# Two transformer-like layers on one core: free VectorE time for waiting shift adds, and two more joined gelus

## The chip, the cores and the metric

The kernel runs on one core of a Trainium2 chip. The metric is the device time of one execution in microseconds (us), the median of several runs. The engines are named as in the profile: PE (TensorE), PEld (its weight loads), ACT (ScalarE), DVE (VectorE), POOL (GpSimd) and SP, which here only issues DMAs.

## The reference

The input x is 2048 rows of 512 in bf16. Four blocks are applied, A, B, A, B, with the same weights both times; A and the B after it are called a layer, so there are layer 0 and layer 1.

```python
x = x + A(layernorm(x), wq, wk, wv, wo)
x = x + B(layernorm(x), w1, w2, w3, w4)      # and both once more

def A(x, ...):       # 32 query heads of 16, one key head and one value head
    q = (x @ wq) in 32 heads; k = x @ wk; v = x @ wv
    p = softmax(q @ k.T / 4)
    return (p @ v, heads side by side) @ wo

def B(x, ...):
    h = gelu(layernorm(x) @ w1)
    hs = (four quarters of h, shifted by 1, -1, 2, -2 rows) @ w2
    x1 = x + hs
    return x1 + gelu(layernorm(x1) @ w3) @ w4      # w3: 512 x 1792, w4: 1792 x 512
```

The exponentials are the bulk: 2 layers x 32 heads x 2048 x 2048 of them.

## The kernel before, in words

**Tiles and chunks.** The 2048 rows are 16 tiles of 128. Queries go in chunks (`CHUNKS`): four of 4 tiles in layer 0; 4, 4, 4, 2 and 2 tiles in layer 1. A chunk is written (layer, number). The scores of one half of a block of four heads against one block of keys are a "half", 128 partitions by 1024 numbers; there are 2048 of them in all, 1024 to a layer.

**Two ways for a half.** As a *unit* (`declare_unit`): PE makes two banks of scores (L1127), ACT takes exp of them (L1170), and PE multiplies by the values (`add_pv`, L1281). As a *pair* (`declare_pair`): PE makes two banks, one after the other, and DVE turns each into the bits of an approximate exponential with a multiply and add into a 16-bit integer (L1190). The approximation is the weighted sum of three such exponentials, J, J + 43 and J + 86 in integer steps (`STEP`). The additions are *shifts* (L1227): a `tensor_scalar` on 16-bit integers in SBUF, which POOL or DVE can do. A shift usually does two rows at once, the second term of the newest pair and the third term of the one before, 2048 numbers per partition. PE then makes three value passes for a pair, where a unit has one. There are `N_J` = 5 J slots.

**Side work.** All else is side work: projections, layer norms, the mixer (W1, gelu, W2) and the MLP (W3, gelu, W4). It is declared for a whole chunk when the last half of the chunk is done (`chunk_end`) and is spread under the next chunk's halves. `PACE` sets how densely its matmuls may begin.

**The gelus.** ACT holds one set of functions at a time, so it loads a table between exp and gelu. A chunk has two gelu episodes, one after W1 (L1586) and one after W3 (`gelus`, L1681), each a load, the gelus and a load back. For a chunk in `JOINED`, `mlp` stops behind W3 and remembers itself in `self.kept`; the next chunk's `mixer_in` then runs its own gelu and the kept one in one episode, and only afterwards declares the kept chunk's W4 matmuls (`mlp_out`) and the layer norm, keys and values that they allow for layer 1 (`next_kv`). Before, three chunks of layer 1 are joined and none of layer 0.

**Layer 0 to layer 1.** Layer 1's first chunk begins on the keys it has: 7 blocks against key tiles 0 to 5, then 6 to 10 (`EARLY`), with partial sums put aside. The rest waits for the last rows of layer 0. The queries of (1,0) and (1,1) are made by `qproj`, whose copies go through SP's queue.

**The order.** Nothing is scheduled on the chip. While the kernel is built, a planner (`Plan`) plays the execution through: each operation has a duration (`dur`), a priority (lower goes first) and predecessors. Whenever an engine is free in that play, `_pick` chooses an operation that is ready, and `_place` puts it at the end of the engine's list. On the chip, each engine then runs its list in order with semaphore waits. The planner's figures (latencies `LAT`, `DRAIN`, durations, `port` for the SBUF port that DVE and POOL share) thus decide the order and nothing else. `roll` is its idea of PE's clock: it looks at activity in windows of 3.4133 us. `MOODS` are sets of rules (how eager pairs and side work are); the string `TEMPER` names one mood for each stretch of 12.5 us of the play.

**Where a shift goes.** `shift_op` decides when the shift is declared, often before it can start: if the rows that POOL has been given and that are not yet placed sum to less than `ADDS` (4, in some moods 5 or 6), POOL gets it, else DVE. A shift on DVE takes the place of its pair in `self.pairs`, on which `assign` counts unfinished pairs (`MAX_PAIRS`, 2) before it gives another half to DVE. 

Of the kernel before, what the change touches and what calls it, by code (L numbers as in the profile page):

```python
# [27 lines left out]
class Op:  # L28
    __slots__ = ("eng", "emit", "preds", "npend", "succ", "dur", "prio", "seq", "ready", "start",
                 "end", "take", "give", "dma", "out", "pos", "sem", "vc", "side", "placed", "pe", "feeds", "port", "parts", "after", "entry", "weight", "qop")  # L30


class Plan:
# [4 lines left out]

    LAT = {"PE": 0.06, "ACT": 0.045, "DVE": 0.045, "POOL": 0.1, "SP": 0.1}

    DRAIN = {"ACT": 0.15, "DVE": 0.085, "POOL": 0.0}
    SELF = 0.035
    MARGIN = 0.15
    SWITCH = 0.103
    WAVE = 0.006
    WINDOW = 3.4133
    WARM = 0.40
    STAY = 0.36
# [22 lines left out]
    LEAD = 0.4  # L71
    JOIN = 0.7
    LEFT = 1
    HORIZON = 1.0

    def __init__(self, nc, pool_banks):
# [32 lines left out]
    def op(self, eng, emit, reads=(), writes=(), dur=0.1, prio=None, take=None, give=None,  # L109
# [7 lines left out]
        o.after = after  # L117
        o.feeds = o.qop = None
        o.seq = len(self.ops)
# [75 lines left out]
    def roll(self, t):  # L195
        w = int(t / self.WINDOW)
        while self.window < w:
            ask = self.STAY if self.warm else self.WARM
            self.warm = self.activity[-1] >= ask * self.WINDOW * 2400.0
            self.window += 1  # L200
            self.activity.append(0.0)
# [7 lines left out]
    def _pick(self, eng, t, dense=False):  # L209
# [66 lines left out]
        if o.take is not None:  # L276
            got = bank
            self.pool = [x for x in self.pool if x[1] not in got]
            o.take.bank = got[0] if o.take.n == 1 else got
            for b in got:  # L280
                last = self.pool_last.get(b)
                if last is not None:
                    o.preds.add(last)
        return o

# [89 lines left out]
    def _place(self, o, t):  # L375
# [14 lines left out]
        elif o.eng == "PE":  # L390
# [11 lines left out]
            o.dur = end - t  # L402
            o.end = end + 0.17
            self.free_at["PE"] = t + 0.015 if len(o.pe) > 3 else end
# [39 lines left out]
    def run(self, pump):  # L444
        while True:
            if not self.events:
                if pump(self.now):
                    continue
                break
            t = heapq.heappop(self.events)  # L450
            while self.events and self.events[0] <= t + 1e-9:
                heapq.heappop(self.events)
            self.now = max(self.now, t)
            again = True
            while again:
                again = pump(self.now)
                for e in ENGINES:
                    if self.free_at[e] <= self.now + 1e-9:
                        o = None
                        if e == "PE" and self.now >= self.pe_end - 1e-9 and self.idle():  # L460
                            o = self._pick(e, self.now, dense=True)
                            if o is None:
                                self.filler()
                        if o is None:
                            o = self._pick(e, self.now)
                        if o is None and e == "PE" and self.now >= self.pe_end - 1e-9 and self.left \
                                and self.filler is not None:
                            heapq.heappush(self.events, self.now + 0.25)
                        if o is not None:
                            self._place(o, self.now)  # L470
                            again = True
# [107 lines left out]
class Kernel:  # L579
# [12 lines left out]
    STEP = 43  # L592
    ADDS = 4
    PARTS = (0.3203125, 0.25390625, 0.201171875)
# [3 lines left out]
    CALM_END = (2, 1)  # L598
    JOINED = ((1, 0), (1, 1), (1, 2))
    LATE_OT = 6  # L600
# [15 lines left out]
    MOODS = (  # L616
        (0.55, 3.0, 1.0, 3.0, 0.45, 0.7, 2, 4, 0.0),
        (0.53, 2.5, 0.8, 3.0, 0.45, 0.7, 2, 5, 0.0),
        (0.57, 3.5, 1.2, 3.3, 0.45, 0.7, 2, 4, 8.0),
        (0.52, 3.0, 1.5, 2.0, 0.6, 0.7, 2, 5, -6.0),  # L620
        (0.55, 2.0, 1.0, 3.0, 0.3, 1.0, 2, 4, 0.0),
        (0.55, 4.0, 0.7, 4.0, 0.45, 0.5, 2, 4, 0.0),
        (0.55, 3.0, 1.0, 3.0, 0.45, 0.7, 1, 4, 20.0),
        (0.55, 3.0, 1.5, 2.5, 0.6, 1.0, 3, 5, -15.0),
        (0.60, 3.0, 0.6, 3.0, 0.2, 0.4, 2, 4, 0.0),
        (0.50, 2.7, 1.1, 2.8, 0.5, 0.8, 2, 4, 0.0),
        (0.55, 3.0, 1.0, 3.0, 0.45, 0.7, 2, 4, 20.0),
        (0.55, 1.0, 1.0, 3.0, 0.45, 0.7, 2, 4, 0.0),
        (0.55, 3.0, 1.0, 3.0, 0.45, 0.7, 2, 5, 0.0),
        (0.55, 3.0, 1.0, 3.0, 0.45, 0.7, 2, 4, -15.0),  # L630
        (0.55, 3.0, 1.5, 3.0, 0.7, 1.2, 3, 6, 0.0),
        (0.57, 2.0, 1.0, 2.0, 0.45, 1.0, 3, 4, 0.0),
    )
    TEMPER = "2007ee7feefe3e77397e7f0ef710ef7e7137eeeef85cf427784ffe15048005003909f1eef04f7ef7e3eee8e77574e04e701e0f9515e5bef20000"

# [293 lines left out]
    def ln_in(self, la, tiles, prio=None):  # L929
# [6 lines left out]
        for part in self.portions(tiles):  # L936
            self.stats(src, part, lambda tb: ("X", tb), prio)
            self.rstd(part, prio)
            for tb in part:
                self.apply(base[0][:, tb % 4, :], src(tb), tb, [("X", tb)], [(base[1], tb % 4)],  # L940
                           0.355, prio)
            n0 = (part[0] % 4) * 128
# [212 lines left out]
    def declare_unit(self, g):  # L1155
# [8 lines left out]
        def fpe(e):  # L1164
            ins = None
            for j, h in enumerate(hs):
# [5 lines left out]
                                                       ACTF.Exp, scale=0.25),  # L1172
                         writes=[L, ("EA", ea)], dur=0.06 + 1024 / 1200, prio=0, side=False, give=L)
        o.qop = q
# [48 lines left out]
    def shift_op(self, d, f, rows):  # L1223
# [5 lines left out]
            reads=[t for r in rows for t in self.jtag(r - 1)], writes=[t for r in rows for t in self.jtag(r)],  # L1229
            dur=t_x4(1024 * n) if eng == "DVE" else 0.27 + 0.853 * n, prio=2, side=False, port=True,  # L1230
            after=0.0 if eng == "DVE" else 0.07)
        if eng == "DVE":
            self.pairs[-1] = o
        else:
            o.weight = n
            self.adds.append(o)

# [126 lines left out]
    def scale_pair(self, k, n, fin):  # L1364
# [6 lines left out]
        def fx(e):  # L1371
# [11 lines left out]
            self.RZ[:, :, b0:b0 + 2, :].rearrange("p i b z -> p (b z) i").unsqueeze(3).to_broadcast([128, 16, 2, 16])),  # L1383
           reads=[("RZ", b0), ("RZ", b0 + 1)], writes=[("RZE",)], dur=0.72, prio=fin, port=True)
        op("PE", fx, reads=[("RZE",), ("ID",)], writes=[M], pe=tiled(n), prio=fin, take=M)
# [160 lines left out]
    def mixer_in(self, la, c, tiles, tail):  # L1546
# [4 lines left out]
        for part in self.portions(tiles):  # L1551
            self.stats(lambda tb: self.X[:, tb, :], part, lambda tb: ("X", tb), None)
            self.rstd(part, None, both=True)
            for tb in part:
                self.apply(self.Y[:, tb % 6, :], self.X[:, tb, :], tb, [("X", tb)], [("Y", tb % 6)], 0.355, None)
                op("POOL", lambda e, tb=tb: e.tensor_scalar(
                    out=self.ZR[:, tb % 4, :], in0=self.Y[:, tb % 6, :], scalar1=self.SM[:, 1, tb:tb + 1],
                    scalar2=0.0, op0=ALU.mult, op1=ALU.add),
                   reads=[("Y", tb % 6), ("R2", tb)], writes=[("ZR", tb % 4)],
                   dur=0.71, prio=self.QUICK, port=True)  # L1560
            i0 = part[0] - tiles[0]
# [71 lines left out]
    def mlp(self, la, tiles, tail):  # L1633
# [12 lines left out]
        for tb in tiles:  # L1646
            op("POOL", lambda e, tb=tb: e.tensor_tensor(out=self.X[:, tb, :], in0=self.Y[:, tb % 6, :],  # L1647
                                                       in1=self.X[:, tb, :], op=ALU.add),
               reads=[("Y", tb % 6)], writes=[("X", tb)], dur=1.3, port=True)
        for f in range(14):  # L1650
# [97 lines left out]
```

## Time and profile before

| | us |
|---|---|
| median of 3 runs | 1467.19 |
| lowest and highest | 1467.02, 1468.6 |
| profiled execution, its own time | 1468.02 |
| its span from first to last instruction | 1466.2 |

| engine | busy us | share of the span |
|---|---|---|
| PE | 1436.7 | 98% |
| ACT | 1398.3 | 95% |
| DVE | 1306.2 | 89% |
| POOL | 1119.0 | 76% |

ACT runs 1401 exps, DVE 1294 halves of pairs (647 pairs) and 153 shifts, POOL 526 shifts. ACT has 26 table loads of 1.283 us each. The mean granted clock of PE is 0.994; two stretches ran at half clock.

A line of the groups gives the source line, engine, operation, what is written and read, and the count; then the time in which the group was busy, the mean length of one in ns, and the idle time just ahead of its members with what ended it. A line of the waits gives who waited, for whom, the total in us, how often, and the longest. In the windows each engine's busy time is followed by its instruction count.

### The profile page before, as it was taken

How to read it: one execution, taken by the hardware profiler on the slowest of the kernel's cores; microseconds unless marked ns; L12 is line 12 of the kernel's file. 1: busy time of each engine (PE TensorE's matmuls, PEld its weight loads, DVE VectorE, ACT ScalarE, POOL GpSimd, SP SyncE). 2: the span in 40 equal slices, each digit the busy share in tenths (PEclk: the TensorE clock that was granted, in tenths of full speed). 3: DMA queues.
4: the chain of work that ended last, by engine and by line, in shares of the span. 5: the costliest groups of instructions: out<-in, count | busy, mean ns of one | idle time of the engine just before them, and what ended most of it. 6: DMA issues, size and time to landing. Idle time of an engine off the chain costs nothing.

```text
span 1466.2 us, 64989 instructions
## 1 busy us (share of the span) xinstructions
PE 1436.7 (98%) x29592; PEld 637.1 (43%) x29592; DVE 1306.2 (89%) x2350; ACT 1398.3 (95%) x1487; POOL 1119.0 (76%) x822
## 2 busy tenths in 40 slices
PE   8999999999999999999999999999999999999999
PEld 3344334444334444434444444444444444545555
DVE  8999999999899989999987889999998998988863
ACT  7999999999899999999989999999999999999952
POOL 2878888888789879887874689878887888868741
PEclk9999999999899999999999999999999999999999
DMA  6100100001000000000000000010000000000000
GB/s 218 26 10 5 20 6 6 7 5 20 6 4 7 6 5 6 16 10 4 3 3 3 3 10 11 6 20 5 6 14 13 8 6 14 7 14 13 9 15 24
DMA packets 32660, 21.73 MB, mean 15 GB/s; under 512 B 13056, under 2 KB 31872, under 8 KB 32384
## 3 DMA queue, kind: packets, MB, share of 16 engines
q1 hardware_dynamic: 32384, 17.57, 5.2%
q8 instruction: 231, 3.78, 1.1%
q14 instruction: 45, 0.37, 0.1%
HBM read 7.90 MB, written 2.10 MB: 7 GB/s over the span
## 4 chain that ended last, share of the span: by engine, by line
ACT 62%; PE 30%; DVE 5%; POOL 2%; issue 1%; DMA 0%; POOLq 0%
ACT EA L1170 59%; PE PB L1127 9%; PE PB L720 9%; PE PB L1281 9%; DVE J L1190 2%; ACT G L1681 2%; POOL J L1227 1%; PE PB L918 1%; ACT L1170 1%; DVE ST L834 1%; PE PB L1051 1%; ACT GP L1586 1%; DVE J L1227 0%; PE PB L975 0%; DVE G L1666 0%
## 5 line engine op out<-in xcount | busy, mean ns | idle before, releaser
L1170 ACT ACTIVATE EA<-PB 128x1024 bf16<-128x1024 f32 x1401 | 1290.2, 1162 | 13.1 <-PE PB L1127 12.5
L1227 POOL TENSOR_SCALAR J<-J 128x2048 uint16<-128x2048 uint16 (+1 forms) x526 | 953.8, 1813 | 241.9 <-DVE J L1227 113.9
L1190 DVE TENSOR_SCALAR J<-PB 128x512 uint16<-128x512 f32 x1294 | 830.1, 681 | 70.1 <-PE PB L1127 65.2
L1127 PE MATMUL PB<-QT,KT 32*128 32x512 bf16 (+1 forms) x4608 | 604.8, 361 | 11.1 <-ACT EA L1170 4.1
L1281 PE MATMUL PB<-J,VD 128*32 128x256 bf16 (+1 forms) x8676 | 414.2, 265 | 7.5 <-POOL J L1227 4.1
L1281 PE MATMUL PB<-EA,VP 128*32 128x256 bf16 (+1 forms) x6324 | 355.9, 266 | 1.5 <-DVE J L1190 0.6
L1127 PEld LDWEIGHTS PB<-QT,KT 32*128 32x128 bf16 x4608 | 162.4, 91 | 384.7 <-ACT EA L1170 289.8
L1281 PEld LDWEIGHTS PB<-J,VD 128*32 128x32 bf16 x8676 | 187.6, 95 | 143.0 <-issue 94.6
L1281 PEld LDWEIGHTS PB<-EA,VP 128*32 128x32 bf16 x6324 | 145.8, 95 | 156.3 <-issue 140.4
L720 PE MATMUL PB<-ZT,W 128*32 128x512 bf16 (+2 forms) x2816 | 168.2, 342 | 0.4 <-DVE ZT L927 0.2
L1227 DVE TENSOR_SCALAR J<-J 128x2048 uint16<-128x2048 uint16 (+1 forms) x153 | 109.5, 717 | 7.1 <-POOL J L1227 6.6
L720 PE MATMUL PB<-W,G 128*32 128x512 bf16 x1624 | 104.5, 381 | 0.2 <-ACT G L1681 0.2
L1666 DVE CAST G<-PB 128x512 bf16<-128x512 f32 (+2 forms) x126 | 72.1, 579 | 11.1 <-PE PB L720 9.2
L720 PEld LDWEIGHTS PB<-ZT,W 128*32 128x32 bf16 x2816 | 63.0, 96 | 36.2 <-issue 23.5
L854 POOL TENSOR_TENSOR SM<-SM,MH 128x2 f32<-128x2 f32 (+1 forms) x69 | 50.6, 738 | 20.8 <-DVE SM L856 11.0
L1681 ACT ACTIVATE G<-G 128x1792 bf16<-128x1792 bf16 x29 | 47.0, 1684 | 19.6 <-DVE G L1666 19.6
L720 PEld LDWEIGHTS PB<-W,G 128*32 128x32 bf16 x1624 | 37.2, 96 | 39.4 <-issue 13.2
L1647 POOL TENSOR_TENSOR X<-Y,X 128x512 bf16<-128x512 bf16 x32 | 39.0, 1227 | 8.3 <-DVE Y L1629 5.8
L834 DVE BATCH_NORM_STATS2 ST<-X 128x6 f32<-128x512 bf16 x64 | 42.8, 677 | 1.6 <-DMA X<-in_A_x_dram 1.2
L1321 DVE CAST ACCF<-PB 128x512 bf16<-128x512 f32 (+1 forms) x65 | 40.0, 615 | 2.5 <-PE PB L1281 2.4
L720 PE MATMUL PB<-WO,OT 128*32 128x512 bf16 x512 | 37.8, 381 | 0.9 <-issue 0.9
L1707 DVE TENSOR_TENSOR OUTB<-PB,X 128x512 bf16<-128x512 f32 x16 | 11.0, 688 | 27.7 <-PE PB L720 27.7
(106 smaller groups left out, 745.2 us busy)
## 6 DMA issues: line engine op xcount, KB each, us to landing
OT<-ACCF SPq DMA_DIRECT2D x432, 8.0 KB, 1.8
W<-in_B_w_dram SPq DMA_DIRECT2D x2, 1792.0 KB, 15.0
X<-in_A_x_dram SPq DMA_DIRECT2D x8, 256.0 KB, 5.4
QT<-QS SPq DMA_DIRECT2D x32, 64.0 KB, 2.5
out_dram<-OUTB SPq DMA_DIRECT2D x16, 128.0 KB, 1.7
OT<-ACCF SPq DMA_DIRECT2D x112, 4.0 KB, 2.2
W<-in_B_w_dram SPq DMA_DIRECT2D x2, 512.0 KB, 9.6
WQ<-in_A_wq_dram SPq DMA_DIRECT2D x1, 512.0 KB, 4.9
```

Of the source, the lines that this page charges most:

```text
L720: ins = e.matmul(self.PB[32 * g:32 * g + 32, bank, 0:n], lhsT=lhsT[:, 32 * g:32 * g + 32], rhs=rhs, start=start, stop=stop, tile_position= ...
L834: op("DVE", lambda e, tb=tb: e.bn_stats(self.ST6[:, tb, :], src(tb)), reads=[tagf(tb)], writes=[("ST", tb)], dur=0.606, prio=prio)
L854: op("POOL", lambda e: e.tensor_tensor(out=out, in0=src, in1=self.MH[:, 0, a:b], op=ALU.pow), reads=tags + [("MH",)], writes=tg(r), dur=0. ...
L1127: ins = e.matmul(self.PB[:, bank, j * n:(j + 1) * n], lhsT=self.KT[32 * h:32 * h + 32, la, (kb + j) * 128:(kb + j + 1) * 128], rhs=self.QT ...
L1170: o = q.feeds = op("ACT", lambda e: e.activation(self.EA[:, ea, :, :], self.PB[:, L.bank[0]:L.bank[0] + 2, :], ACTF.Exp, scale=0.25), writ ...
L1190: o = op("DVE", lambda e, i=i, L=L: e.tensor_scalar(out=self.J[:, 3 * s, i * 512:(i + 1) * 512], in0=self.PB[:, L.bank, :], scalar1=128 * ...
L1227: o = self.pl.op(eng, lambda e: e.tensor_scalar(out=self.J[:, d, :], in0=self.J[:, f, :], scalar1=float(self.STEP), scalar2=1.0, op0=ALU.a ...
L1281: ins = e.matmul(self.PB[32 * x:32 * x + 32, A.bank, p * hw:p * hw + hw], lhsT=v[:, la, kb + j, :], rhs=ap[:, i, j * w + u * hw:j * w + u ...
L1321: self.last_copy = op("DVE", lambda e: e.tensor_copy(acc, self.PB[:, A.bank, 0:n]), writes=[ac] + am, dur=t_ps(n), prio=0, side=False, give=A)
L1647: op("POOL", lambda e, tb=tb: e.tensor_tensor(out=self.X[:, tb, :], in0=self.Y[:, tb % 6, :], in1=self.X[:, tb, :], op=ALU.add), reads=[(" ...
L1666: op("DVE", lambda e, f=f, L=L: e.tensor_copy(self.G2[:, f, 0:n], self.PB[:, L.bank, 0:n]), writes=[L] + [(x, f, i) for x in ("G2", "GE") ...
L1681: self.pl.op("ACT", lambda e, i=i: e.activation(self.G2[:, :, i * 128:(i + 1) * 128], self.G2[:, :, i * 128:(i + 1) * 128], ACTF.Gelu_appr ...
```

## The change

1. A new `borrow`: when DVE has nothing else to do in the planner's play, POOL is busy and the shared port comes free within `LULL` = 0.45 us, DVE takes the oldest ready shift out of POOL's queue.
2. `ADDS` goes up by 2 in every mood: POOL may be given up to 6 (or 7, 8) unplaced rows before a shift is bound to DVE.
3. `JOINED` takes in (0,0) and (0,1).
4. Planner figures: some durations, `LAT` of DVE, `DRAIN` of ACT, the end of a single bank of scores, `JOIN` from 0.7 to 1.3 (the priority at which a unit's scores that aren't urgent join others), and `roll` now moves in quarters of a window (`BINS`).
5. Another `TEMPER`; the two strings agree in 22 of 116 places.

```diff
-    LAT = {"PE": 0.06, "ACT": 0.045, "DVE": 0.045, "POOL": 0.1, "SP": 0.1}
+    LAT = {"PE": 0.06, "ACT": 0.045, "DVE": 0.05, "POOL": 0.1, "SP": 0.1}
-    DRAIN = {"ACT": 0.15, "DVE": 0.085, "POOL": 0.0}
+    DRAIN = {"ACT": 0.11, "DVE": 0.085, "POOL": 0.0}
+    BINS = 4
-    JOIN = 0.7
+    JOIN = 1.3
+    LULL = 0.45
...
     def roll(self, t):
-        w = int(t / self.WINDOW)
+        w = int(t * self.BINS / self.WINDOW)
         while self.window < w:
             ask = self.STAY if self.warm else self.WARM
-            self.warm = self.activity[-1] >= ask * self.WINDOW * 2400.0
+            self.warm = sum(self.activity[-self.BINS:]) >= ask * self.WINDOW * 2400.0
...
+    def borrow(self, t):
+        if self.free_at["POOL"] <= t + 1e-9 or self.port - t > self.LULL:
+            return None
+        h = [o for o in self.heap["POOL"] if o.flex and o.ready <= t + 1e-9]
+        if not h:
+            return None
+        o = min(h, key=lambda o: o.seq)
+        self.heap["POOL"].remove(o)
+        o.eng, o.dur, o.after = "DVE", o.flex, 0.0
+        return o
...
-            o.end = end + 0.17
+            o.end = end + (0.195 if kind == "Q" and act < 200 else 0.17)
...
                         if o is None:
                             o = self._pick(e, self.now)
+                        if o is None and e == "DVE":
+                            o = self.borrow(self.now)
...
-    ADDS = 4
+    ADDS = 6
-    JOINED = ((1, 0), (1, 1), (1, 2))
+    JOINED = ((0, 0), (0, 1), (1, 0), (1, 1), (1, 2))
...
     MOODS = (
-        (0.55, 3.0, 1.0, 3.0, 0.45, 0.7, 2, 4, 0.0),
+        (0.55, 3.0, 1.0, 3.0, 0.45, 0.7, 2, 6, 0.0),
...
-    TEMPER = "2007ee7feefe3e77397e7f0ef710ef7e7137eeeef85cf427784ffe15048005003909f1eef04f7ef7e3eee8e77574e04e701e0f9515e5bef20000"
+    TEMPER = "0184777f99f477e52777e374efe430779ef2771778570177e0083e2004000314093e49710fef799feef443873f1e0ee11705c154031407220200"
...
-            dur=t_x4(1024 * n) if eng == "DVE" else 0.27 + 0.853 * n, prio=2, side=False, port=True,
+            dur=t_x4(1024 * n) if eng == "DVE" else 0.264 + 0.859 * n, prio=2, side=False, port=True,
...
         else:
             o.weight = n
+            o.flex = t_x4(1024 * n)
             self.adds.append(o)
```

The other durations change a little: an exp from 0.06 to 0.0632 plus its 1024 / 1200, a layer norm's application from 0.355 to 0.33, and on POOL the spread of the reciprocals from 0.72 to 0.69, the second norm's scaling from 0.71 to 0.68 and the X add from 1.3 to 1.24.

## The prediction

> **What bounds the kernel now.** The order of reading was: busy shares on the page, then the windows of the span, then the waits, then the chain and the timeline at the one place where ScalarE stands still.
>
> ```profile
> PE 1436.7 (98%) x29592; PEld 637.1 (43%) x29592; DVE 1306.2 (89%) x2350; ACT 1398.3 (95%) x1487; POOL 1119.0 (76%) x822
> ...
> L1170 ACT ACTIVATE EA<-PB 128x1024 bf16<-128x1024 f32 x1401 | 1290.2, 1162 | 13.1 <-PE PB L1127 12.5
> L1227 POOL TENSOR_SCALAR J<-J 128x2048 uint16<-128x2048 uint16 (+1 forms) x526 | 953.8, 1813 | 241.9 <-DVE J L1227 113.9
> L1190 DVE TENSOR_SCALAR J<-PB 128x512 uint16<-128x512 f32 x1294 | 830.1, 681 | 70.1 <-PE PB L1127 65.2
> ...
> L1227 DVE TENSOR_SCALAR J<-J 128x2048 uint16<-128x2048 uint16 (+1 forms) x153 | 109.5, 717 | 7.1 <-POOL J L1227 6.6
> ```
>
> All four compute engines look full, so the shares decide nothing. The windows do:
>
> ```profile
> 36.00:1400.00 1364.00, 1342.22 (x27402) 585.59 (x27400) 1244.36 (x2190) 1347.72 (x1431) 1096.17 (x770) 0.99 0.05 9
> ...
> 300.00:400.00 100.00, 99.03 (x1846) 41.61 (x1846) 89.86 (x163) 97.11 (x103) 77.91 (x61) 0.95 0.06 11
> ...
> 700.00:800.00 100.00, 99.13 (x1964) 44.66 (x1956) 85.56 (x164) 92.22 (x92) 63.20 (x66) 1.00 0.01 3
> ```
>
> The columns are PE, weight loads, DVE, ACT, POOL, then the granted clock. Between 36 and 1400 us ACT is busy 1347.7 of 1364: 16.3 us idle, half of them in 700 to 800. A microsecond of ACT work taken out of this body is nearly a microsecond off the end. DVE has 119.6 us free there and POOL 267.8. PE's 98% counts pipelined spans; the waits show its slack:
>
> ```profile
> PEld PB L1127 <- ACT EA L1170: 287.2, 973, 0.6
> ...
> POOL J L1227 <- DVE J L1227: 111.8, 82, 4.8
> POOL J L1227 <- DVE J L1190: 88.0, 76, 14.3
> DVE J L1190 <- PE PB L1127: 65.2, 145, 1.9
> ...
> PEld PB L1281 <- POOL J L1227: 19.9, 58, 1.4
> ...
> ACT EA L1170 <- PE PB L1127: 8.6, 17, 0.9
> ACT G L1681 <- DVE G L1666: 6.6, 1, 6.6
> ...
> DVE J L1227 <- POOL J L1227: 6.6, 16, 0.9
> ```
>
> (Waiter, awaited, us in total, times, longest.) The score matmuls wait for ACT 287 us in the body; ACT waits for PE 8.6. So ACT is the bound, and what matters is how many of the 2048 units ACT must take (1401) and how many the pairs on DVE take (1294 / 2 = 647).
>
> **The change part by part.** The sum is made against the profiled execution: span 1466.2, its own time 1468.0, which is 0.8 above the median 1467.2.
>
> *Joined gelus, removal.* In layer 0 each chunk now has two gelu episodes on ACT; a joined chunk hands its second to the next chunk's first.
>
> ```profile
> 611.04 1.28 ACT L1586 ACT_TABLE_LOAD   x1
> 612.33 1.91 ACT L1586 ACTIVATE GP<-GP 128x2048 bf16<-128x2048 bf16 x1
> 614.26 1.28 ACT L1170 ACT_TABLE_LOAD   x1
> ```
>
> Chunks (0,0) and (0,1) lose one episode each: 4 loads. The row gives 1.283 us for one, and ACT drains ahead of it: an exp has a span of 1.162 but a pitch of 1290.2 / 1401 = 0.921, so 0.24 of overlap is lost each time. 4 x 1.52 = 6.1 us, all on ACT, on the path. The Trainium skill (ScalarE: Activation LUTs, Terms) puts a load at about 2.7 us, its drain included, which would make 10.8; the same page's section on what the load costs has the 1283 ns of the row. I take the rows: **-6.1**.
>
> *Joined gelus, what moves.* The W4 matmuls, X adds, layer norm, keys and values of (0,1) (`mlp_out`, `next_kv`) leave the stretch after 511 us and go behind the first gelu of (0,2), now at 612. Those of (0,0) move likewise, with much time to spare; in the stretch of (0,1) one set leaves as another comes. The stretch of (0,2) only gains, and it is the tight one (two pieces of the chain, two lines of the timeline):
>
> ```profile
> 734.12 3.10 PE PB L720 x56
> ...
> 763.29 8.59 PE PB L720 x208
> ...
> 772.50 1.70 ACT L1681 ACTIVATE G<-G 128x1792 bf16<-128x1792 bf16 x1 [6.60 <-DVE G L1666]
> 774.12 0.45 PEld L975 LDWEIGHTS PB<-YT,WK 128*32 128x32 bf16 x16 [0.21 <-DVE YT L927]
> ```
>
> Layer 1's first units run ahead on the keys that exist; at 765.9 they are used up, and ACT stands 6.6 us until a gelu can run, exps returning at 778.7, after keys of (0,2) at 774 to 776. Those come from W4 matmuls that follow the gelu at 704.6. Added ahead of that gelu are four tiles of 56 matmuls at 3.10 us = 12.4 us, and some 2 us of keys, transposes and values. Upper bound, if no gap of PE absorbs them: 14.4 us. Lower bound: the gap goes, -6.6. The value taken is **+5**, because the section is also relieved: what lay between 513 and 598 us in front of (0,2)'s own layer norm is gone, so its first gelu can come before 612. On SP's queue the query loads of (1,0) (8 copies, 2.5 us to landing) go later with the keys they are built behind; layer 1's first exp is near 696, which leaves them tens of us. On DVE four adds and four layer norms move too, under DVE's 119.6 free us; on GpSimd three pairs of small operations for the norms (L856 0.28, L854 0.74: 3.1 us), which go ahead of shifts, under its 267.8.
>
> *Shift adds.* Before, a shift that found 4 rows unplaced for GpSimd was bound to DVE when declared, even if it could not start yet. Now 6 may wait, and DVE takes one only when it has nothing and GpSimd is busy. The waits show what this is worth: 82 times GpSimd stood idle (111.8 us) until a shift that DVE had been given was over. A rule speaks against any gain here: the Trainium skill (SBUF — State Buffer, Who interferes with whom) says that such a DVE copy and GpSimd exclude each other for the whole instruction. The rows agree in kind (a GpSimd shift starts within 0.1 us of the DVE one's end) but not in size: 82 shifts at 0.68 us are 56 of the 111.8 us; the other 56 are GpSimd without a ready shift. By the rule alone a returned shift only holds the port longer (1.9 instead of 0.68 us), and the pairs stay at 647: 0. By the rows: if half of the 82 go back, DVE gets 41 x 0.68 = 28 us, and a pair costs it 2 x 830.1 / 1294 = 1.28 us, so 22 more pairs fit; GpSimd needs (41 + 22) x 1.9 = 120 us of the 111.8 + 88.0 it idles. I take half of that, 11, since pair supply also hangs on banks and on PE (DVE waits 65.2 us for scores). Each takes one exp of 0.921 off ACT: **-10.1**. Bounds: +9 (10 pairs fewer, since a shift may now wait behind 3 others, 5.7 us, with five J slots) and -40 (all 82 go back: 44 pairs).
>
> *A borrowed shift's wait.* DVE may sit on a borrowed shift up to `LULL`, 0.45 us, for the port; the row of this wait has 6.6 us in 16, 0.41 each. Behind it queue the next J evacuations, and behind these a PSUM bank for the next scores. 80 borrowings at 0.41 are 33 us, inside DVE's 119.6: nothing while that holds, up to 33 us of DVE (26 pairs fewer at worst) without it. Three more PV passes per pair and a longer GpSimd queue make PE wait more for J: 19.9 us now, perhaps half as much again, under the 287 us that PE waits for ACT.
>
> *Remeasured figures, finer clock windows, new moods.* They change order alone. Two stretches of half clock (0.98 and 0.95 in the windows) coincide with ACT waits of 4.1 us near 390 to 403 and 0.3 at 222. A plan that foresees the gate in quarter windows may lose none or lose others: bounds -4.4 and +4.4, taken **-2.2**, half avoided. Start and tail (9.3 and 42 us of ACT idle) follow the same chains: 0, bounds 3 either way.
>
> Sum: 1468.0 - 6.1 + 5 - 10.1 - 2.2 = 1454.6; minus 0.8 for the median: **1454 us**.
>
> **The rivals.** *GpSimd's port is what binds.* The pairs stay at 647, the rest holds: 1467.2 - 6.1 + 5 - 2.2 = 1464, half of it at the edge of no change. For it: the lock, and POOL's body at 80%. Against: half of the idle time above isn't lock.
>
> *Layer 1's keys come late (slower).* The moved 14.4 us all fall between the gelu now at 704.6 and the keys now at 774, and pairs don't grow: 1467.2 - 6.1 + 14.4 = 1475. For it: the side work there already ends last, and at 763 PE runs 208 of its matmuls without a break. It decides once the gap of 6.6 us grows by more than 6.1 plus what pairs bring. Against: the relief before 598 us.
>
> *DVE's slack is used up well.* 33 more pairs: 30 us instead of 10 off ACT, 1434. Against: DVE would need 42 us more, and its gaps are short waits for scores.
>
> *The borrowing hardly fires.* Where GpSimd's queue rarely exceeds four rows, only tables and order remain; this falls together with the first rival in time.
>
> **How the numbers follow.** Main forecast 0.55, own range 1445 to 1463; port 0.20 at 1464; late keys 0.16 at 1475; more pairs 0.09 at 1434. The range 1439 to 1472 leaves out the better part of the last two and holds the others. About 0.2%, 2.9 us, is what can be told from no change. Faster by more: 0.55 + 0.09 + half of the port case = 0.74. Within: 0.08. Slower: 0.16 plus a little of the main case's bounds = 0.18.
>
> **What would show it.** ACT table loads 26 to 22. EA on ACT from 1401 to about 1390, L1190 from 1294 to about 1316. GpSimd's shifts from 526 to about 550, and its idle time until DVE's shift well below 111.8. ACT's idle time near the layer boundary between 0 and 20 us, about 12 expected. Granted clock 1.00 in all or all but one window. The forecast is wrong if L1190 doesn't rise, if the gap before L1681 near 770 passes 20 us, or if ACT's idle time in the body passes 25.

## The result and the profile after

| | before | after |
|---|---|---|
| median of 6 runs, us | 1467.11 | 1453.51 |
| lowest and highest | 1460.82, 1468.6 | 1452.62, 1455.03 |
| span of the profiled execution | 1466.2 | 1450.8 |
| mean granted clock in it | 0.994 | 1.00 |

The ratio is 0.9928, with a 95% interval of 0.991 to 0.9946. The forecast was 1454, faster.

From the page of the kernel after, the busy time and the groups (L1186 is the exp, L1206 the pairs' conversion, L1243 the shift, which were L1170, L1190 and L1227):

```profile
PE 1425.7 (98%) x29716; PEld 640.2 (44%) x29716; DVE 1321.1 (91%) x2383; ACT 1382.0 (95%) x1471; POOL 1139.6 (79%) x825
...
L1186 ACT ACTIVATE EA<-PB 128x1024 bf16<-128x1024 f32 x1389 | 1279.3, 1159 | 11.2 <-PE PB L1143 10.9
L1243 POOL TENSOR_SCALAR J<-J 128x2048 uint16<-128x2048 uint16 (+1 forms) x529 | 967.2, 1828 | 204.6 <-DVE J L1206 95.8
L1206 DVE TENSOR_SCALAR J<-PB 128x512 uint16<-128x512 f32 x1318 | 844.7, 679 | 49.1 <-PE PB L1143 42.5
...
L1243 DVE TENSOR_SCALAR J<-J 128x2048 uint16<-128x2048 uint16 (+1 forms) x162 | 114.7, 709 | 13.3 <-POOL J L1243 11.8
```

ACT has 12 exps fewer and DVE 12 pairs more (1318 / 2 = 659). The shifts did not move as foreseen: POOL has 3 more and DVE 9 more. The pitch of an exp is the same as before, 1279.3 / 1389 = 0.921. ACT's table loads after are 22, where there were 26:

```profile
L1186 ACT ACT_TABLE_LOAD x10 | 12.8, 1283 | 0.2
L1603 ACT ACT_TABLE_LOAD x8 | 10.3, 1283 | 0.1
L1698 ACT ACT_TABLE_LOAD x3 | 3.8, 1283 | 0.1
L812 ACT ACT_TABLE_LOAD x1 | 1.3, 1283 | 0.7 <-PEq L1750 0.7
```

From the windows after (PE, weight loads, DVE, ACT, POOL, granted clock):

```profile
36.00:1400.00 1364.00, 1345.81 (x27894) 596.27 (x27896) 1270.87 (x2246) 1343.61 (x1425) 1120.54 (x779) 1.00 0.05 9
...
700.00:800.00 100.00, 99.34 (x2006) 45.11 (x1994) 85.79 (x168) 90.30 (x94) 64.23 (x63) 1.00 0.01 3
```

The span ends 15 us earlier, so this fixed window now holds part of the tail; the clock is full throughout, where it was 0.99 before. Windows that end with the last exp, before and then after, compare like with like:

```profile
36.00:1404.54 1368.54, 1346.77 (x27556) 588.30 (x27558) 1246.49 (x2194) 1352.26 (x1435) 1097.22 (x771) 0.99 0.05 9
36.00:1385.94 1349.94, 1332.06 (x27590) 586.85 (x27592) 1259.07 (x2224) 1336.29 (x1419) 1117.17 (x774) 1.00 0.05 9
```

DVE is busy 12.6 us longer in a stretch that is 18.6 us shorter, so its idle time falls from 122 to 91 us. From the waits between 36 and 1400 us after:

```profile
POOL J L1243 <- DVE J L1206: 95.8, 76, 12.7
POOL J L1243 <- DVE J L1243: 69.8, 69, 3.3
...
DVE J L1206 <- PE PB L1143: 41.8, 99, 1.0
...
DVE J L1243 <- POOL J L1243: 11.8, 29, 1.6
```

POOL's idle time until a shift on DVE is over fell from 111.8 to 69.8 us. DVE now waits 41.8 us for scores where it waited 65.2: its gaps were filled. By the groups, the 12 pairs and 9 shifts take 20 us more (844.7 - 830.1 and 114.7 - 109.5); with all its other work DVE is busy 14.9 us longer.

The layer boundary and the tail, from the timeline of ACT after, then the same place of the tail before:

```profile
752.84 1.94 ACT L1186 ACTIVATE EA<-PB 128x1024 bf16<-128x1024 f32 x2 [1.95 <-PE PB L1143]
754.79 1.28 ACT L1698 ACT_TABLE_LOAD   x1
762.23 4.87 ACT L1698 ACTIVATE G<-G 128x1792 bf16<-128x1792 bf16 x3 [6.15 <-DVE G L1683]
...
1393.96 1.06 ACT L1603 ACTIVATE GP<-GP 128x1024 bf16<-128x1024 bf16 x1 [6.72 <-DVE G L1683]
```
```profile
1409.54 1.06 ACT L1586 ACTIVATE GP<-GP 128x1024 bf16<-128x1024 bf16 x1 [3.69 <-DVE G L1666]
```

The boundary costs ACT 1.95 + 6.15 us instead of 6.60. The last gelu after W1 waits 3.0 us longer than before.

### The profile page after: what moved, and what is told of

Same layout as the page of the kernel before. It is cut to its first block, busy times and chain, and to the rows that moved or that the text cites. A ratio compares the mean times of both kernels' runs of the same rounds, so it can differ in the third digit from the quotient of the medians.

```text
span 1450.8 us, 65311 instructions
## 1 busy us (share of the span) xinstructions
PE 1425.7 (98%) x29716; PEld 640.2 (44%) x29716; DVE 1321.1 (91%) x2383; ACT 1382.0 (95%) x1471; POOL 1139.6 (79%) x825
## 4 chain that ended last, share of the span: by engine, by line
PE 49%; ACT 31%; POOL 10%; DVE 7%; issue 2%; DMA 0%; POOLq 0%
ACT EA L1186 29%; PE PB L1143 16%; PE PB L1298 16%; PE PB L736 15%; POOL J L1243 9%; DVE J L1206 4%; DVE J L1243 1%; ACT G L1698 1%; PE PB L934 1%; POOL SM L870 1%; POOL ZR L1573 1%; DVE ST L850 0%; PE PB L1067 0%; ACT GP L1603 0%; PE PB L991 0%
## 5 line engine op out<-in xcount | busy, mean ns | idle before, releaser
L1186 ACT ACTIVATE EA<-PB 128x1024 bf16<-128x1024 f32 x1389 | 1279.3, 1159 | 11.2 <-PE PB L1143 10.9
L1243 POOL TENSOR_SCALAR J<-J 128x2048 uint16<-128x2048 uint16 (+1 forms) x529 | 967.2, 1828 | 204.6 <-DVE J L1206 95.8
L1206 DVE TENSOR_SCALAR J<-PB 128x512 uint16<-128x512 f32 x1318 | 844.7, 679 | 49.1 <-PE PB L1143 42.5
L1143 PE MATMUL PB<-QT,KT 32*128 32x512 bf16 (+1 forms) x4608 | 592.4, 360 | 8.4 <-ACT EA L1186 4.2
L1298 PE MATMUL PB<-EA,VP 128*32 128x256 bf16 (+1 forms) x6256 | 360.6, 265 | 2.6 <-DVE J L1206 0.6
L1243 DVE TENSOR_SCALAR J<-J 128x2048 uint16<-128x2048 uint16 (+1 forms) x162 | 114.7, 709 | 13.3 <-POOL J L1243 11.8
L870 POOL TENSOR_TENSOR SM<-SM,MH 128x2 f32<-128x2 f32 (+1 forms) x69 | 54.5, 793 | 21.3 <-DVE SM L872 13.6
L1664 POOL TENSOR_TENSOR X<-Y,X 128x512 bf16<-128x512 bf16 x32 | 39.0, 1224 | 14.9 <-DVE Y L1646 13.0
L736 PE MATMUL PB<-W,GP 128*32 128x512 bf16 x512 | 34.0, 380 | 0.4 <-ACT GP L1603 0.4
```

The source lines that it names most:

```text
L736: ins = e.matmul(self.PB[32 * g:32 * g + 32, bank, 0:n], lhsT=lhsT[:, 32 * g:32 * g + 32], rhs=rhs, start=start, stop=stop, tile_position= ...
L870: op("POOL", lambda e: e.tensor_tensor(out=out, in0=src, in1=self.MH[:, 0, a:b], op=ALU.pow), reads=tags + [("MH",)], writes=tg(r), dur=0. ...
L1143: ins = e.matmul(self.PB[:, bank, j * n:(j + 1) * n], lhsT=self.KT[32 * h:32 * h + 32, la, (kb + j) * 128:(kb + j + 1) * 128], rhs=self.QT ...
L1186: o = q.feeds = op("ACT", lambda e: e.activation(self.EA[:, ea, :, :], self.PB[:, L.bank[0]:L.bank[0] + 2, :], ACTF.Exp, scale=0.25), writ ...
L1206: o = op("DVE", lambda e, i=i, L=L: e.tensor_scalar(out=self.J[:, 3 * s, i * 512:(i + 1) * 512], in0=self.PB[:, L.bank, :], scalar1=128 * ...
L1243: o = self.pl.op(eng, lambda e: e.tensor_scalar(out=self.J[:, d, :], in0=self.J[:, f, :], scalar1=float(self.STEP), scalar2=1.0, op0=ALU.a ...
```

## The experiments

The theory was: ACT's exps and loads set the time, DVE's idle time covers what DVE is given more, and half-clock stretches add to the kernel before. The rivals were that the saved loads are hidden elsewhere, that DVE or the shared port is the bound, and that the new order as a whole, not its parts, carries the gain. Times below "at full clock" are of runs with a granted clock of 1.00: 1453.1 for the kernel after (four runs) and 1461.4 for the kernel before (median of 28 runs beside the experiments).

### e1: the loads put back, the order kept

```diff
+        def first(e):
+            e.activation(self.TINY[:, 0:1], self.ONES[:, 0:1], ACTF.Exp)
+            return e.activation(self.G2[:, :, 0:128], self.G2[:, :, 0:128], ACTF.Gelu_apprx_tanh)
...
-            self.pl.op("ACT", lambda e, i=i: e.activation(
+            self.pl.op("ACT", first if apart and i == 0 else lambda e, i=i: e.activation(
...
-                self.gelus(kept[2], [("GX", f) for f in range(4)])
+                self.gelus(kept[2], [("GX", f) for f in range(4)], kept[0] == 0)
```

> The order of the changed kernel, kept in every place. In the two joined episodes of layer 0 a one-column exp stands ahead of the first kept gelu, so that ACT loads the exp table and the gelu table once more in each: 4 loads more, 26 in all. Borrowed shifts are issued from a line of their own, so that the profile counts them apart (104 of the 162 on DVE in the order as built). If ACT is the bound and the loads that joining saved were on the path: 4 x 1.283, two tiny exps of some 0.2 and the drains, 5.5 to 7 us over the changed kernel's 1453.5, so 1459 to 1460.5. If the wait at the layer boundary or the tail hides them: 1453 to 1455.

Measured: 1462.0 (1460.0 to 1463.3), above the range expected; at full clock 1460.4 (three runs), within it, and 7.3 over the kernel after at full clock. From the timeline of ACT in e1, one of the two episodes, and the boundary; then the same episode in the kernel after:

```profile
395.69 1.91 ACT L1609 ACTIVATE GP<-GP 128x2048 bf16<-128x2048 bf16 x1
397.62 1.28 ACT L1703 ACT_TABLE_LOAD   x1
398.91 0.21 ACT L1703 ACTIVATE TINY<-ONES 128x1 bf16<-128x1 bf16 x1
399.12 1.28 ACT L1704 ACT_TABLE_LOAD   x1
400.42 1.70 ACT L1704 ACTIVATE G<-G 128x1792 bf16<-128x1792 bf16 x1
402.02 3.27 ACT L1707 ACTIVATE G<-G 128x1792 bf16<-128x1792 bf16 x2
405.31 1.28 ACT L1188 ACT_TABLE_LOAD   x1
...
768.28 4.87 ACT L1707 ACTIVATE G<-G 128x1792 bf16<-128x1792 bf16 x3 [6.15 <-DVE G L1689]
```
```profile
395.51 1.91 ACT L1603 ACTIVATE GP<-GP 128x2048 bf16<-128x2048 bf16 x1
397.33 4.86 ACT L1698 ACTIVATE G<-G 128x1792 bf16<-128x1792 bf16 x3
402.20 1.28 ACT L1186 ACT_TABLE_LOAD   x1
```

From the first gelu to the load behind the last, one episode takes 9.62 us in e1 and 6.69 in the kernel after: 2.9 more, of which 0.2 are the one-column exp. At the boundary e1 is 768.28 - 762.23 = 6.05 us behind, with the same wait of 6.15, so the four loads alone cost about 5.6 us there. They are on the path, and the wait at the boundary absorbs none of them: what PE and DVE hand over there comes later by as much. The rest arises behind 1200 us: there the two profiled runs are 6.2 us apart, and at the last exp 8.0. As e8, further down, also falls back by 1.8 us in that part and has no load more than the kernel after, the loads are not shown to be the reason; what makes it stays open. The groups of e1 also count the borrowed shifts (their own line, L1256) apart from those that were bound to DVE:

```profile
L1256 DVE TENSOR_SCALAR J<-J 128x2048 uint16<-128x2048 uint16 (+1 forms) x104 | 72.8, 700 | 11.7 <-POOL J L1245 10.7
L1245 DVE TENSOR_SCALAR J<-J 128x2048 uint16<-128x2048 uint16 (+1 forms) x58 | 42.3, 733 | 2.2 <-POOL J L1245 1.8
```

Shifts bound to DVE fell from 153 to 58, and 104 borrowed ones took their place.

### e2, e5, e6, e8: does DVE's idle time cover anything?

The first three add work to each borrowed shift in the order of the kernel after; e8 takes work away from DVE.

```diff
             def lent(e):
+                e.tensor_scalar(out=self.J2[:, :], in0=self.J[:, rows[0] - 1, 0:640], scalar1=float(self.STEP), scalar2=1.0, op0=ALU.add, op1=ALU.mult)      # e2
+                e.bn_stats(self.ST2[:, :], self.J[:, rows[0] - 1, 0:256].bitcast(dt.bfloat16))      # e5
                 ins = e.tensor_scalar(out=self.J[:, d, :], in0=self.J[:, f, :], scalar1=float(self.STEP), scalar2=1.0, op0=ALU.add, op1=ALU.mult)
+                e.bn_stats(self.ST2[:, self.nlent % 8, :], self.ONES[:, 0:256])      # e6
                 return ins
...
-            op("DVE", lambda e, tb=tb: e.bn_stats(self.ST6[:, tb, :], src(tb)),
+            op("DVE", lambda e, tb=tb: e.bn_stats(self.ST6[:, tb, :], src(tb)[:, 0:256]),      # e8
```

In e2 as it ran, the addition stood ahead of the shift, not behind it as the expectation says.

> The order of the changed kernel. Each borrowed shift is followed on DVE by one more addition of the same kind on 640 numbers into a spare row, by the row of the 1024 form (0.42 us) some 0.25 us each, so about 26 us of DVE and of the shared port more, spread over the 104 borrowings. If DVE's idle time (93 us in the body) covers borrowing, as the prediction has it: under 4 us more than 1453.5. If DVE or the port has become the bound: 10 to 26 us more.

> The order of the changed kernel. Ahead of each of the 104 borrowed shifts DVE does a bn_stats over 256 numbers into a spare row, an operation that GpSimd ran beside in the earlier runs, of about 0.3 us, as long as the extra addition of the run before it (0.30 us of DVE each, 27 us in all at the end). If DVE's place in its own list is what binds (what stands behind a borrowed shift is late by as much): again 20 us or more over 1453.5. If it was the shared port, with GpSimd held up: under 8 us more.

> The order of the changed kernel. The bn_stats over 256 numbers of the run before (0.42 us each, 104 of them) now stands behind the borrowed shift on DVE and not ahead of it, so that the shift's own readers on PE are not held up, only what DVE does next. If DVE's next turning of scores is what is late: again 25 us or more over 1453.5. If it was the shift's result that PE waited for: under 10 us more.

> The order of the changed kernel, with the 96 bn_stats of the layer norms taken over 256 of the 512 columns, which leaves out half of the statistics; each falls from 0.68 to 0.42 us, 25 us of DVE less. If DVE is as tight downwards as upwards (27 to 32 us of DVE added cost as much in time): 10 us or more below 1453.5. If ACT is the bound and DVE counts only when it is late against its list: at most 4 us less.

| | DVE's busy time against 1321.1, us | time, us | against 1453.5 | granted clock of the runs |
|---|---|---|---|---|
| e2, ahead, on the shared port | +31.7 | 1480.4 | +26.9 | 0.993 to 0.999 |
| e5, ahead, bn_stats | +37.4 | 1485.7 | +32.2 | 0.989 to 0.994 |
| e6, behind, bn_stats | +27.2 | 1471.3 | +17.8 | 0.995 to 0.998 |
| e8, statistics halved | -19.1 | 1453.4 | -0.1 | 1.00 |

The groups of e2, e5, e6 and e8, the exp and the added or shortened operation:

```profile
L1188 ACT ACTIVATE EA<-PB 128x1024 bf16<-128x1024 f32 x1389 | 1289.5, 1070 | 27.9 <-PE PB L1145 25.2
...
L1256 DVE TENSOR_SCALAR J<-J 128x640 uint16<-128x640 uint16 x104 | 39.1, 376 | 12.1 <-POOL J L1245 10.5
```
```profile
L1188 ACT ACTIVATE EA<-PB 128x1024 bf16<-128x1024 f32 x1389 | 1292.2, 1070 | 35.6 <-PE PB L1145 31.8
...
L1256 DVE BATCH_NORM_STATS2 ST<-J 128x6 f32<-128x256 bf16 x104 | 44.0, 423 | 12.3 <-POOL J L1245 10.9
```
```profile
L1188 ACT ACTIVATE EA<-PB 128x1024 bf16<-128x1024 f32 x1389 | 1288.8, 1071 | 20.2 <-PE PB L1145 17.7
...
L1258 DVE BATCH_NORM_STATS2 ST<-ONES 128x6 f32<-128x256 bf16 x104 | 43.6, 419 | 0.0
```
```profile
L1187 ACT ACTIVATE EA<-PB 128x1024 bf16<-128x1024 f32 x1389 | 1280.1, 1155 | 12.1 <-PE PB L1144 11.4
...
L851 DVE BATCH_NORM_STATS2 ST<-X 128x6 f32<-128x256 bf16 x64 | 25.9, 413 | 3.0 <-DMA X<-in_A_x_dram 2.6
```

In e2, e5 and e6 the exps, of which there are as many, wait more for PE (idle 27.9, 35.6 and 20.2 instead of 11.2), and their mean length falls from 1159 to 1070: an exp that starts late overlaps its predecessor less (by 0.24 us on average in the kernel after, by 0.14 in e2), so the group's busy time grows by 9 to 13 us without any work. With 93 us of idle time in the body (1364.0 less 1270.87), DVE could not take some 30 us more without most of it showing at the end. Some of that is half clock: across the half-clock windows of the profiled runs ACT falls behind by about 4 us in e2, 13 in e5 and 4 in e6. But the runs of e2 at 0.998 and 0.999 still took 1478.5 and 1478.2. So the theory's "covered by idle time" falls. By their expectations e2 and e5 speak for DVE, or its place in its list, as what binds, e8 speaks for ACT, and e6 lies between its two cases.

The port is not needed to explain it. A bn_stats runs beside GpSimd, as the timeline of the kernel before shows, DVE inside the time of POOL:

```profile
754.85 1.17 POOL L1647 TENSOR_TENSOR X<-Y,X 128x512 bf16<-128x512 bf16 x1
...
755.29 0.68 DVE L834 BATCH_NORM_STATS2 ST<-Y 128x6 f32<-128x512 bf16 x1
```

and e5 costs as much as e2: 32.2 us for 37.4 of DVE against 26.9 for 31.7, and with the half-clock parts left out some 24 us each in the profiled runs. (Also, 32 of the 96 bn_stats of the kernel before lie wholly within a shift of POOL, and a two-row shift of POOL takes 1.90 to 1.91 us with a bn_stats beside it and without.) e6 parts the cost: 17.8 us when only what DVE does next is late, and up to 14.4 more, part of it half clock, when the shift's readers on PE are late as well (44 us of bn_stats in both). The other way nothing is gained: 19 us of DVE taken away bring 0.1. The reading that fits is that ACT is the bound and DVE is tight in one direction: each engine follows a list in which DVE's result is due just when PE needs it. One difference stands beside the direction, though: e8 takes its time from the layer norms, which are side work, and not from the borrowed shifts.

### e3 and e7: the kernel before, kept at full clock

```diff
+    KEEP_WARM = ((211.0, 217.0), (381.0, 388.5))      # e7: ((382.0, 385.5),)
...
         def fpe(e):
             ins = None
+            if not first and any(a <= box[0].start < b for a, b in self.KEEP_WARM):
+                self.dot(e, A.bank, 512, self.NIL, self.ONES, False, False)
```

> The kernel before in its own order, with a matmul of zeros (512 columns, 0.21 us) added into the running sum ahead of each value pass that was planned for two stretches of 6 to 7.5 us, ahead of where the granted clock fell to half (near 219 and 390 us of the span). If the half clock is what ACT waited for there (4.1 and 0.3 us): clock 1.00, 3 to 5 us less than the kernel before in runs in which that one went cold. If the order makes ACT wait there, whatever the clock: no change, or the 5 us of added PE work as a loss.

> The kernel before in its own order, with zero matmuls ahead of only 7 value passes (1.5 us of PE in all) just ahead of the stretch near 390 us, where the earlier kept-warm run had 34 (7.2 us). If the four half-clock windows cost the 5 us by which the kernel's runs at clock 0.995 are above those at 1.00, and the 34 passes gave that back as PE time: clock 0.998 or more in every run, 1461.5 to 1463. If PE's added time counts whole wherever it stands, and 7 are too few: as before, 1466 to 1467 in most runs.

e3: 1466.2 (1465.3 to 1467.5), clock 0.999 or 1.00 in every run. e7: 1462.7 (1461.7 to 1464.0), clock 1.00 in ten of twelve runs and never under 0.998. The windows of the kernel before, 3.4 us each, show what happens there; the number behind PE's busy time is its matmuls:

```profile
382.60:386.00 3.40, 3.40 (x84) 1.65 (x72) 3.40 (x8) 3.40 (x6) 3.16 (x4) 1.00 0.09 17
386.00:389.40 3.40, 2.98 (x37) 0.99 (x36) 3.04 (x7) 3.33 (x5) 3.08 (x5) 1.00 0.00 0
389.40:392.80 3.40, 3.40 (x44) 1.13 (x44) 3.40 (x7) 2.76 (x4) 3.24 (x3) 0.62 0.00 0
392.80:396.20 3.40, 3.40 (x51) 0.78 (x43) 2.18 (x5) 2.64 (x3) 3.22 (x4) 0.50 0.08 15
396.20:399.60 3.40, 3.40 (x37) 0.77 (x29) 1.54 (x4) 2.28 (x3) 1.31 (x2) 0.50 0.05 10
399.60:403.00 3.40, 3.40 (x64) 1.77 (x62) 1.73 (x3) 2.05 (x2) 2.19 (x2) 0.50 0.02 5
```

One thin window, 37 matmuls, is followed by 13.7 us of half clock, in which ACT's share falls to 2.05 of 3.40. The same part of the span in e7:

```profile
300.00:400.00 100.00, 99.35 (x1952) 43.35 (x1948) 92.42 (x167) 99.70 (x107) 79.64 (x63) 1.00 0.06 11
```

ACT has 2.6 us more there than in the kernel before. Exp for exp, e7's profiled run is 0.8 us ahead behind the stretch near 220 us, which did not go cold in it, and 5.3 us ahead behind the one near 390. Sorted by clock, the runs of the kernel before beside the experiments have medians of 1461.4 at 1.00 (28 runs), 1466.5 at 0.995 (30), 1467.4 at 0.994 (15) and 1468.8 at 0.993 (8). Seven zero passes hold the first level at 1.3 us of cost; thirty-four lose again what they save. So half clock costs the kernel before 5 us in its usual run. Where e3 left it open, with the loss by 34 passes as large as the gain, e7 settles it for the clock: its highest of twelve runs is 1464.0, while 7 of the 17 runs of the kernel before beside it lie between 1465.6 and 1468.7. (The medians of the two, 1462.7 and 1462.3, don't differ, since the other ten were at 0.998 or above without help.)

### e4: borrowing off, everything else kept

```diff
     def borrow(self, t):
-        if self.free_at["POOL"] <= t + 1e-9 or self.port - t > self.LULL:
-            return None
+        return None
```

> The changed kernel without borrowing, all figures and the string of moods as in the changed kernel. The order as built has 1431 exps on ACT in place of 1389, 617 pairs, 564 shifts on POOL and 86 on DVE. If the pairs carry the time: 42 exps of 0.921 are 39 us, so about 1492, and more where PE or ACT idles because the string was made for another play. If borrowing matters little: within 10 us of 1453.5.

Measured: 1517.1 (two runs). From its groups:

```profile
L1185 ACT ACTIVATE EA<-PB 128x1024 bf16<-128x1024 f32 x1431 | 1317.4, 1160 | 16.9 <-PE PB L1142 16.0
...
L1205 DVE TENSOR_SCALAR J<-PB 128x512 uint16<-128x512 f32 x1234 | 795.1, 682 | 141.5 <-PE PB L1142 135.7
```

42 exps more account for 39 of the 64 us; DVE idles 141.5 us ahead of turning scores, 135.7 of them until PE has made these. That is no price of borrowing: the string of moods was made for another play, in which one changed choice changes all later ones; s3 below, with `ADDS` as before and a string of its own, does without borrowing in 1472.8. A part can't be judged with the string kept.

### s1 to s4: the parts, each with a string of its own

The string of moods was looked for anew in one way for four kernels: s1 all of the change, s2 without joining in layer 0, s3 without borrowing and with `ADDS` as before, s4 the kernel before.

```diff
 s2 -    JOINED = ((0, 0), (0, 1), (1, 0), (1, 1), (1, 2))
 s2 +    JOINED = ((1, 0), (1, 1), (1, 2))
 s3 +        return None      # in borrow; ADDS and MOODS as in the kernel before
 all -    TEMPER = "..."
 all +    TEMPER = (another string)
```

> The changed kernel with another string of moods, looked for anew by one and the same method for this run and the three beside it: stretch by stretch, keeping the dozen strings that had done most so far. The order as built has 1403 exps, 645 pairs, 517 shifts on POOL, 162 on DVE (104 borrowed). If the number of exps alone sets the time: 14 exps of 0.921 over 1453.5, 1466. If the fit of the order counts for more: ACT idles more, and it is later than that.

> The changed kernel without joining in layer 0, string of moods looked for anew in the same way. 1395 exps, 653 pairs, 519 shifts on POOL, 164 on DVE (99 borrowed), 26 loads. If joining is worth the 6.1 us of its loads and the rest follows the exps: s1 - 8 x 0.921 + 6 = about 1 us less than s1. If the moved W4 work costs more than the loads, well below s1.

> The changed kernel without borrowing and with the former limit of 4 rows for GpSimd, joining and figures kept, string of moods looked for anew in the same way. 1410 exps, 638 pairs, 529 shifts on POOL, 143 on DVE. If borrowing is what brings the pairs: 7 exps more than s1, 6 us later than s1. If pairs come from the fit of the string, within 5 us of s1 either way.

> The kernel before with a string of moods looked for anew in the same way: old figures, no borrowing, no joining in layer 0. 1395 exps, 653 pairs, 537 shifts on POOL, 143 on DVE. If the parts of the change carry its gain: 8 to 15 us later than s1. If the search of the string carries it, this lies within 5 us of s1.

| | exps | time, us | at full clock |
|---|---|---|---|
| s1, all of it | 1403 | 1474.3 | 1470.3 |
| s2, without joining | 1395 | 1468.4 | 1468.2 |
| s3, without borrowing | 1410 | 1472.8 | 1471.4 |
| s4, the kernel before | 1395 | 1474.6 | 1474.5 |
| before, given string | 1401 | 1466.2 | 1461.4 |
| after, given string | 1389 | 1453.5 | 1453.1 |

With strings looked for alike, all of the change is worth 4 us at full clock (s1 against s4), nothing in the medians, and borrowing 1 us at full clock (s1 against s3; three runs each). So s3 and s4 both lie within 5 us of s1, the case in which by their expectations the string makes the difference. s2, without the joining and with 8 exps fewer, is 2.1 us below s1 at full clock, near the 1.4 that 8 x 0.921 for the exps less 6 for the loads make. The four lie within 6.3 us of each other at full clock, and their strings are worse than the two given ones by 13 us for s4 and 17 for s1. What a string brings is thus larger than what separates the parts, and with one string for each the share of borrowing in the 12 pairs is not settled; s4 reaches 653 pairs without it, and still ends late. So the count of exps does not set the time alone either. The planner's figures (point 4 of the change) were not tried apart from the rest. The rival that the new order as a whole carries the gain thus stands, but for the loads (e1) and the half clock (e7), which are shown one by one.

## Why the prediction was right, and where only its total was

The kernel before at full clock is e7, whose profiled span was 1461.0, with 1.3 us of zero passes in its time. Read from the traces of e7 and after, up to the last exp and behind it, and from the medians:

| step | foreseen | found |
|---|---|---|
| loads of layer 0 | -6.1 | -5.3 in ACT's busy time, 5.1 of it the loads; 5.6 by e1 |
| 12 pairs more | -10.1 | -10.1 (exps, 1289.4 to 1279.3) |
| moved W4 work, boundary | +5 | +2.2 (ACT's idle time up to the last exp) |
| granted clock | -2.2 | -5.3 (13.6 less 8.3 at full clock) |
| start and tail | 0 | +3.1 |
| zero passes in e7, spread of single runs | | +1.9 |
| sum | -13.4 | -13.5, of a measured -13.6 |

The lines of e7 for it:

```profile
L1171 ACT ACTIVATE EA<-PB 128x1024 bf16<-128x1024 f32 x1401 | 1289.4, 1162 | 8.3 <-PE PB L1128 7.5
...
36.00:1399.20 1363.20, 1341.75 (x27579) 587.94 (x27582) 1248.04 (x2194) 1351.71 (x1435) 1098.01 (x771) 1.00 0.05 9
```

**The loads** were right in place, and in size to within a microsecond. The rows' 1.28 held, and the larger figure of the Trainium skill (ScalarE: Activation LUTs, Terms), about 2.7 us for a load, did not: e1 shows 1.28 for each, and 2.9 us for two loads with their drains and the one-column exp. Of the 0.24 us of overlap that the working adds to each load, e1, whose loads stand between gelus, shows about 0.1.

**The pairs** were right in number and wrong in mechanism. The step "half of the 82 go back" to GpSimd failed: POOL has 529 shifts instead of 526. What happened is that 95 shifts fewer were bound to DVE ahead of time, and 104 were taken by DVE in gaps of its own, so DVE's total rose by 9 shifts and 12 pairs, 20 us by the groups, out of its idle time. That the count of 11 came so near is therefore luck. And 11 of the 12 pairs lie in the second 1024 halves, those of layer 1: the first 1024 take 692 exps before and 691 after, although 49 of the 104 borrowings lie there. By the Trainium skill (SBUF — State Buffer, Who interferes with whom), VectorE in a two-port mode and GpSimd block each other for a whole instruction. These shifts bear it out: of some 110 us of them on DVE before, 10 lie beside one of POOL's. The estimate of no pair more, which the working drew from it, was off by 12 pairs, but not because shifts went back to the port's slower user. Whether borrowing or the new string found these 11 pairs is open, as s1 and s3 show.

**The moved work** cost less than +5: ACT's idle time at the boundary is 8.10 us instead of 6.60, and 12.0 instead of e7's 10.3 in all of the second 1024 halves. The stretch before was relieved by more than assumed: the first gelu of (0,2) runs at 555 us, 607 in e7, and the second at 689, 701 in e7. The exps return at 768.4, 773.4 in e7. (In the kernel before it is 612, 706 and 778.7, but 5.3 us of these are half clock further ahead.) That the joining did this is argued, not shown, for the string moves it as much: the gap at the boundary is 13.20 us in s1, with the joining, and 13.67 in s4, without. The rival of late keys, which would have decided at a gap grown by more than 6.1, did not come about in the given order.

**The clock** was mis-sized. I read the loss from the waits that the profile gives to ACT (4.4 us) and took half. The new order keeps the clock at 0.998 or above in all six runs, and the runs of the kernel before differ by 5 us between 1.00 and 0.995, some of it in lost overlap of the exps that no wait shows. The reason given, that the plan foresees the gate in quarter windows, is not borne out: s1 has them and ran at 0.995 to 0.997 in five of eight runs; s4 has not and ran at 0.999 or 1.00 in all eight. So far as these runs show, staying warm is a property of the one order, and to have it is luck.

**The tail** was put at 0, with a bound of 3; it took the whole bound: from the last exp to the end it is 64.9 us, 61.8 in e7, as the last gelu after W1 waits 6.72 instead of 3.69 us for DVE's copies of the MLP ahead of it. This wait, too, goes with the string: 3.17 us in s1, 5.99 in s2.

**A borrowed shift's wait** was costed at nothing under 119.6 us of idle DVE time. That reason was wrong, though the term did not show, since the order was built with the borrowings in it and the wait came to 11.8 us, not 33: e2, e5 and e6 give 0.65 to 0.86 us, half clock included, for every us by which DVE is busy beyond its list.

**The sum** closes in the traces. From e7 to the kernel after, up to the last exp, ACT's busy time falls by 15.4 us (5.1 for four loads, 10.1 for the exps), its idle time rises from 11.5 to 13.7, and the tail grows by 3.1: 10.2 us, the difference of the spans. At full clock the medians differ by 8.3, which leaves 1.9 for e7's zero passes (1.3) and the spread of single runs. The clock adds the rest of the 13.6. So the total of 1454 came out though single terms were off by up to 3 us: the clock gave 3.1 more than foreseen and the boundary took 2.8 less, but the tail took 3.1 and the loads gave 0.8 less. That these cancel is luck, and 5.3 of the 13.6 us are the clock's, in an order that happened to keep it.

**The signs named** came as said in the loads (22), the exps (1389 against 1390), L1206 (1318 against 1316), the boundary (8.1 us, between 0 and 20, 12 expected), GpSimd's idle time (69.8) and the clock; GpSimd's shifts did not (529 against 550). Of the rivals, the one in which borrowing hardly fires is out (104), and so is the one with 33 more pairs. The port's, that the pairs stay at 647, is out for the order as given (659).

## What to carry to other kernels

Where the order is fixed ahead, idle time is not slack: 27 to 37 us more on an engine that idled for 93 cost 18 to 32, and 19 us less on it brought nothing; cost an edit by whether the order was built with it in, and look for gains on the engine whose waits are shortest. Before a gain of a per cent is put down to an edit, sort the runs by granted clock and find the thin window ahead of a half-clock stretch; a few matmuls of zeros there show at once what it costs. When a change comes with a searched setting, a part can be judged only with a setting searched for it at equal effort, and the spread of that search is the error bar.

## What the runs showed of the hardware

One window of 3.4 us with 37 matmuls, where the five ahead of it had 64 to 87, was followed by half clock for four such windows; near 220 us one with 38 was followed by one at half clock. That did not happen in every run of one and the same program: of 87 runs of the kernel before, 28 had a clock of 1.00 and 53 one of 0.995 or lower. Seven passes of zeros, 1.5 us of PE, kept it at 0.998 or above in twelve runs. An exp's busy time in the profile also hides waiting: with ACT starved in small steps the group of the same 1389 exps was busy for 1289.5 us instead of 1279.3.
